# Block attention ahead of an MoE: scores taken per head on half of TensorE's rows, 128 queries of one head at a time, in a new order of units

## The chip, the core and the metric

The kernel runs on one core of a Trainium2 chip. The metric is device time in microseconds of one execution, from launch to end; before the change it was 1011.18 us, the median of three runs (1010.61 to 1013.1). TensorE (PE) multiplies and transposes, VectorE (DVE) and ScalarE (ACT) read its results from PSUM, GpSimd (POOL) works in SBUF alone, and SyncE (SP) issues nearly all DMAs.

## The reference

Three layers follow each other: attention with a mask in blocks of 64, a mixture of 8 experts in which each expert takes 288 tokens, and a bilinear layer. The change touches the first.

```python
B, H, S, D = 4, 8, 576, 64
scores = q @ k.T / sqrt(D)                  # per batch and head, 576 x 576
mask = (pos_q // 64) >= (pos_k // 64)       # nine blocks of 64; a block sees itself and those before
attn = softmax(where(mask, scores, -1e9))
x = (attn @ v)                              # to [B*S, H*D] = [2304, 512]
# then: experts relu(x @ w1[e]) @ w2[e] for the 288 tokens that each expert takes,
# then: (x @ w_a) * (x @ w_b) @ w_out
```

Precision is kept by splitting: a product in fp32 is made of three in the faster type fp32r, high by high, high by low and low by high, so `kh`, `kl` are the two parts of the transposed keys and `qh`, `ql` those of the queries. Transposes and the product with v stay in fp32.

## The kernel before

The attention works on 16 pairs of heads, one pair (`n`) per step, with the two heads' 64 features side by side on the 128 partitions. A pair's work is cut into units: `k`, `q`, `t` transpose keys and queries on PE and copy them out on ACT (lines 83 to 107); `sk`, `sp` split them on POOL (lines 114 to 120); `S0` to `S8` take the scores of one block of 64 queries, `E0` to `E8` their exponentials; `A0` to `A6` transpose the 25 tiles of 128x128 (line 172) and copy them to SBUF (line 174); `P0` to `P4` multiply with v (line 190); `ev` copies the result to `xT` (lines 195 and 196). `S` is three matmuls (line 149) and a maximum on DVE (line 150). Its stationary tile `qh[:,i,:]` is block-diagonal: the 64 queries of head 0 stand over the first 64 rows and those of head 1 over the others, with zeros elsewhere, so one matmul over all 128 rows gives 64 queries of both heads, and half of the array multiplies zeros. Blocks 0 and 1 are done in fp32 (line 137).

The order in which the units are issued is the string `SEQ`, walked once per step. `S` and `E` are of pair n, `A`, `P`, `ev` of pair n-1 and the transposes and splits of pair n+1, so a step overlaps three pairs. Each engine executes what it gets in that order. `w` stands for one piece of side work (constants for the routing, then the conversion of three weight arrays on DVE, three passes for each of 36 tiles, lines 797 to 801, with DMAs in and out), and `x` for a piece of what follows a finished batch of four pairs (`rr`, `lgm`, `lgt`, `first`: reciprocal sums and routing logits). PSUM's eight banks hold three `tr` tiles, three `s` tiles and one `pv` tile of two banks, which also takes the scores of the ninth block. The string `ACT` says which groups of `A` are copied by ACT; the others go to DVE.

After the last pair the routing of the first expert runs alone, and then the experts and the bilinear layer follow.

Of the kernel before, what the change touches and what calls it, by code (L numbers as in the profile page):

```python
# [13 lines left out]
ACT='46531'  # L14
# [3 lines left out]
SEQ='k A0 S0 e8 A1 S1 q E1 A2 w A3 S2 P0 t E0 E2 w w x A4 S3 E3 A5 w S6 S4 E4 P1 w sk x A6 w P2 P3 P4 ev E6 S5 E5 S7 S8 w E7 x sp'  # L18
def attention(ctx, tc, q, k, v, w_gate, xT, r_all, logits, idf, side, first):
# [3 lines left out]
    nc=tc.nc  # L23
# [3 lines left out]
    NB=S//64  # L27
    NC=B*S//128
    cst=ctx.enter_context(tc.tile_pool(name="acst",bufs=1))
    raw=ctx.enter_context(tc.tile_pool(name="araw",bufs=2))  # L30
    wk=ctx.enter_context(tc.tile_pool(name="awk",bufs=2))
    ps=ctx.enter_context(tc.tile_pool(name="aps",bufs=2,space=PSUM))
    QH,QL,QF,AA,VV=[],[],[],[],[]
    NF=2
    for i in range(2):
        t=cst.tile([128,NF,128],F32,name=f"qf{i}")
        nc.gpsimd.memset(t,0.0)
        QF.append(t)
        for l,nm in ((QH,"qh"),(QL,"ql")):
            t=cst.tile([128,NB,128],F32R,name=f"{nm}{i}")  # L40
            nc.gpsimd.memset(t.bitcast(F32),0.0)
            l.append(t)
    for i in range(2):
        t=cst.tile([128,25,128],F32,name=f"A{i}")
        AA.append(t)
    nc.vector.memset(AA[0],0.0)
    for i in range(4):
        t=cst.tile([128,5,2,64],F32,name=f"v{i}")
        nc.vector.memset(t[64:128,4],0.0)
        VV.append(t)  # L50
    one=cst.tile([128,1],F32,name="one")
    nc.gpsimd.memset(one,1.0)
    nc.scalar.activation(cst.tile([128,1],F32,name="tab"),one,AF.Exp)
    wg=cst.tile([128,HP,32],F32,name="wg")
    nc.gpsimd.memset(wg,0.0)
    L=cst.tile([128,NC,128],F32,name="L")
    RT=cst.tile([128,B,HP,NB],F32,name="RT")
    st={}
    off=[0]
    for i in range(NB): off.append(off[-1]+i//2+1)  # L60
    order=[(i,j) for j in range(5) for i in range(2*j,NB)]
    joff=[order.index((2*j,j)) for j in range(5)]

    def load(n):
        b,hp=divmod(n,HP)
        def ld(t,src):
            for h in range(2):
                nc.sync.dma_start(t[:,0:4,h,:],src[b,2*hp+h,0:512,:].rearrange("(i p) d -> p i d",p=128))
            nc.sync.dma_start(t[0:64,4,:,:],src[b,2*hp:2*hp+2,512:576,:].rearrange("h p d -> p h d"))
        for nm,src in (("k",k),("q",q)):  # L70
            t=raw.tile([128,5,2,64],F32,name=nm+"r")
            ld(t,src)
            st[nm,n]=t
        ld(VV[n%4],v)

    def t_units(n):
        def mk():
            st['kh',n]=wk.tile([128,S],F32R,name="kh")
            st['kl',n]=wk.tile([128,S],F32R,name="kl")
            st['qT',n]=wk.tile([128,S],F32,name="qT")  # L80
            st['kT',n]=wk.tile([128,S],F32,name="kT",bufs=2)
        def evk(p,a,b):
            nc.scalar.copy(st['kT',n][:,a:b],p)
        def first():
            if ('kh',n) not in st: mk()
        def km():
            first()
            p=ps.tile([128,512],F32,name="tr",bufs=3)
            for i in range(4):
                nc.tensor.transpose(p[:,128*i:128*i+128],st['k',n][:,i].rearrange("p h d -> p (h d)"),idf)  # L90
            evk(p,0,512)
        def tl():
            first()
            p=ps.tile([128,512],F32,name="tr",bufs=3)
            nc.tensor.transpose(p[:,0:64],st['k',n][0:64,4].rearrange("p h d -> p (h d)"),idf[0:64,0:64])
            nc.tensor.transpose(p[:,64:128],st['q',n][0:64,4].rearrange("p h d -> p (h d)"),idf[0:64,0:64])
            evk(p[:,0:64],512,576)
            nc.scalar.mul(st['qT',n][:,512:576],p[:,64:128],0.125)
        def qm():
            first()  # L100
            p=ps.tile([128,512],F32,name="tr",bufs=3)
            for i in range(4):
                nc.tensor.transpose(p[:,128*i:128*i+128],st['q',n][:,i].rearrange("p h d -> p (h d)"),idf)
            nc.scalar.mul(st['qT',n][:,0:512],p,0.125)
            for h in range(2):
                s=slice(64*h,64*h+64)
                nc.scalar.mul(QF[n%2][s,:,s],p[s,0:64*NF].rearrange("p (i d) -> p i d",d=64),0.125)
        def sp():
            qT=st.pop(('qT',n)); qh,ql=QH[n%2],QL[n%2]
            for h in range(2):  # L110
                s=slice(64*h,64*h+64)
                src=qT[s].rearrange("p (i d) -> p i d",d=64)
                eng=nc.vector if n==0 and h==0 else nc.gpsimd
                eng.tensor_tensor(qh[s,:,s],src,one[s,:,None].to_broadcast([64,NB,64]),op=ALU.mult)
                eng.tensor_tensor(ql[s,:,s],src,qh[s,:,s].bitcast(F32),op=ALU.subtract)
        def sk():
            kT=st['kT',n]; kh,kl=st['kh',n],st['kl',n]
            eng=nc.gpsimd if n else nc.vector
            eng.tensor_tensor(kh,kT,one.to_broadcast([128,S]),op=ALU.mult)
            eng.tensor_tensor(kl,kT,kh.bitcast(F32),op=ALU.subtract)  # L120
        return dict(q=qm,t=tl,sp=sp,k=km,sk=sk)

    def s_units(n):
        b,hp=divmod(n,HP)
        def grp(i):
            W=64*(i+1)
            def f():
                if i==0:
                    st['sm',n]=wk.tile([128,NB],F32,name="sm")
                    st['mx',n]=wk.tile([128,NB],F32,name="mx")  # L130
                mx=st['mx',n]
                kh,kl=st['kh',n],st['kl',n]
                qh,ql,qf,kT=QH[n%2],QL[n%2],QF[n%2],st['kT',n]
                if i<NF:
                    p=ps.tile([128,512],F32,name="s",bufs=3)
                    view=p[:,:W]
                    nc.tensor.matmul(p[:,:128],qf[:,i,:],kT[:,:128],start=True,stop=True)
                    parts=[]
                elif W<=512:
                    p=ps.tile([128,512],F32,name="s",bufs=3)  # L140
                    parts=[(p[:,:max(W,256)],0,max(W,256))]
                    view=p[:,:W]
                else:
                    p=ps.tile([128,2,512],F32,name="pv",bufs=1)
                    parts=[(p[:,c,:W//2],c*W//2,W//2) for c in range(2)]
                    view=p[:,:,:W//2]
# [3 lines left out]
                nc.vector.tensor_reduce(mx[:,i:i+1],view,axis=AX.X if W<=512 else AX.XY,op=ALU.max,negate=True)  # L150
                st['view',n,i]=view
            def g():
                A=AA[n%2]; sm=st['sm',n]; mx=st['mx',n]
                view=st.pop(('view',n,i))
                o=A[:,off[i]:off[i+1],:].rearrange("p a b -> p (a b)")[:,:W]
                if W>512: o=o.rearrange("p (a b) -> p a b",a=2)
                nc.scalar.activation(o,view,AF.Exp,bias=mx[:,i:i+1],accum_out=sm[:,i:i+1])  # L157
                if i==NB-1:
                    nc.vector.tensor_scalar(sm,sm,1e-9,None,op0=ALU.add)
                    nc.vector.reciprocal(RT[:,b,hp,:],sm)  # L160
            return f,g
        return [grp(i) for i in range(NB)]

    def at_units(n):
        def grp(g):
            def f():
                if g==0: st['AT',n]=wk.tile([128,2,25*64],F32,name="AT")
                A,AT=AA[n%2],st['AT',n]
                blk=order[4*g:4*g+4]; nb=len(blk)
                p=ps.tile([128,512],F32,name="tr",bufs=3)  # L170
                for m,(i,j) in enumerate(blk):
                    nc.tensor.transpose(p[:,128*m:128*m+128],A[:,off[i]+j,:],idf)  # L172
                o=AT[:,:,256*g:256*g+64*nb].rearrange("p h (i d) -> p h i d",d=64)
                (nc.scalar.copy if str(g) in ACT else nc.vector.tensor_copy)(o,p[:,:128*nb].rearrange("p (i h d) -> p h i d",h=2,d=64))
            return f
        return [grp(g) for g in range(7)]

    def pv_units(n):
        b,hp=divmod(n,HP)
        cut=[0,320,576]  # L180
        def main(j):
            def f():
                if j==0: st['pv',n]=ps.tile([128,2,512],F32,name="pv",bufs=1)
                p,AT,vv=st['pv',n],st['AT',n],VV[n%4]
                for c in range(2):
                    a,e=max(128*j,cut[c]),cut[c+1]
                    if a>=e: continue
                    for h in range(2):
                        o=64*joff[j]+a-128*j
# [51 lines left out]
    for u in ('k','q','t','sk','sp'): T[u]()  # L241
# [3 lines left out]
    for n in range(N+1):  # L245
        if n+2<N: load(n+2)
# [20 lines left out]
    for f in pend+batch_units(B-1): f()  # L267
# [590 lines left out]
```

## Time and profile before

| of the profiled execution | value |
|---|---|
| its own time | 1013.26 us |
| span from first to last instruction | 1011.5 us |
| mean granted clock of TensorE | 0.976 of 2.4 GHz |
| PE busy | 954.3 us, 94% |
| DVE busy | 711.2 us, 70% |
| ACT busy | 439.9 us, 43% |
| POOL busy | 206.4 us, 20% |

The profiled execution took 2.1 us more than the median of the runs. Its span is 1.8 us shorter than its time. The attention fills the first 231 us, the routing of the first expert lies at 231 to 285 us, and what remains is the experts and the bilinear layer, in which PE is the busy engine. A row's duration is the latency of one instruction; instructions of an engine overlap, so the cost of one in a stream is read from the distance between the starts of neighbours.

### The profile page before, as it was taken

The numbers are of one execution on the slowest core, as the hardware profiler recorded it, in microseconds if no ns is written. First come the engines' busy times: TensorE is split into PE (matmuls) and PEld (weight loads), VectorE is DVE, ScalarE is ACT, GpSimd is POOL, SyncE is SP. The second block draws the span as 40 slices with busy tenths as digits, with TensorE's granted clock in tenths as the row PEclk, the third lists the DMA queues.
The fourth block names the chain that finished last, engine by engine and source line by source line (L and its number), as shares of the span: only waits on it lengthen the run. The fifth ranks groups of instructions, "written<-read, shape, count | busy, mean of one in ns | idle before, by whom it ended". The sixth has DMA issues, their size and how long they took to land.

```text
span 1011.5 us, 20472 instructions
## 1 busy us (share of the span) xinstructions
PE 954.3 (94%) x7741; PEld 893.9 (88%) x7741; DVE 711.2 (70%) x1627; ACT 439.9 (43%) x1108; POOL 206.4 (20%) x215
## 2 busy tenths in 40 slices
PE   6998999988499999999999999999999999999996
PEld 5776877766398999999999999999999999999996
DVE  6889899896687876776767767766767776535421
ACT  5775777753363344225323522442253235325321
POOL 8766566622100020011001100200110011101001
PEclk9999899997599999999999999999999999999999
DMA  6687787633784245025304611440352046215300
GB/s 141 177 238 201 195 228 205 186 103 137 223 260 133 59 125 160 21 75 162 94 12 118 180 44 43 147 130 23 97 160 73 12 119 190 67 52 160 84 12 24
DMA packets 134563, 123.14 MB, mean 122 GB/s; under 512 B 64320, under 2 KB 97088, under 8 KB 134464
## 3 DMA queue, kind: packets, MB, share of 16 engines
q1 hardware_dynamic: 131392, 112.32, 38.8%
q0 software_dynamic: 3072, 9.51, 3.0%
q8 instruction: 61, 1.00, 0.4%
q14 instruction: 38, 0.31, 0.1%
HBM read 102.85 MB, written 18.95 MB: 120 GB/s over the span
## 4 chain that ended last, share of the span: by engine, by line
PE 80%; DVE 10%; DMA 5%; ACT 2%; issue 2%; POOL 1%; SPq 0%; POOLq 0%; DVEq 0%; ACTq 0%
PE h L637 13%; PE h L638 12%; PE h L639 12%; PE acc L638 8%; PE acc L637 8%; PE acc L639 8%; PE tr L172 4%; PE s L149 3%; PE pv L190 3%; DMA xo<-xs,idx 3%; PE m L438 2%; DVE mx L150 1%; PE pv L149 1%; PE h L746 1%; DVE cf L801 1%
## 5 line engine op out<-in xcount | busy, mean ns | idle before, releaser
L637 PE MATMUL acc<-th,spl 128*128 128x288 f32 x640 | 191.8, 300 | 0.4 <-ACT th L688 0.3
L638 PE MATMUL acc<-tl,spl 128*128 128x288 f32 x640 | 189.2, 296 | 0.5
L639 PE MATMUL acc<-th,spl 128*128 128x288 f32 x640 | 189.5, 296 | 0.0
L624 DVE TENSOR_TENSOR spl<-raw,spl 128x512 fp32r<-128x512 f32 x224 | 153.0, 689 | 29.3 <-ACT spl L623 23.3
L623 ACT CAST spl<-raw 128x512 fp32r<-128x512 f32 x224 | 137.4, 620 | 35.6 <-PE acc L639 28.8
L525 POOL DMA_INDIRECT xo<-xs,idx x24 | 25.6, 1067 | 492.2 <-DVE cg L534 448.1
L638 PEld LDWEIGHTS acc<-tl,spl 128*128 128x128 f32 x640 | 120.9, 189 | 1.7 <-DVE tl L689 1.5
L637 PEld LDWEIGHTS acc<-th,spl 128*128 128x128 f32 x640 | 120.6, 188 | 0.9 <-ACT th L688 0.9
L639 PEld LDWEIGHTS acc<-th,spl 128*128 128x128 f32 x640 | 120.5, 188 | 0.0
L688 ACT CAST th<-h 128x288 fp32r<-128x288 f32 x96 | 38.3, 399 | 182.3 <-DVE h L686 181.0
L637 PE MATMUL h<-y,wah 128*128 128x288 f32 x384 | 116.1, 302 | 0.0
L637 PE MATMUL h<-y,wbh 128*128 128x288 f32 x384 | 115.1, 300 | 0.0
L638 PE MATMUL h<-y,wbh 128*128 128x288 f32 x384 | 113.4, 295 | 0.0
L639 PE MATMUL h<-y,wal 128*128 128x288 f32 x384 | 113.4, 295 | 0.0
L638 PE MATMUL h<-y,wah 128*128 128x288 f32 x384 | 113.1, 295 | 0.0
L639 PE MATMUL h<-y,wbl 128*128 128x288 f32 x384 | 113.0, 294 | 0.0
L681 ACT COPY ta<-h 128x288 f32<-128x288 f32 x96 | 38.3, 399 | 158.8 <-PE h L639 158.8
L686 DVE TENSOR_TENSOR h<-h,ta 128x288 f32<-128x288 f32 x96 | 44.4, 463 | 87.9 <-PE h L639 85.9
L637 PE MATMUL h<-xh,spl 128*128 128x288 f32 x256 | 79.7, 311 | 3.4 <-ACT xh L570 3.4
L157 ACT ACTIVATE A<-s,mx 128x128 f32<-128x128 f32 (+7 forms) x128 | 64.0, 504 | 38.3 <-DVE mx L150 37.3
L638 PE MATMUL h<-xl,spl 128*128 128x288 f32 x256 | 76.8, 300 | 1.1 <-DVE xl L571 1.1
L639 PE MATMUL h<-xh,spl 128*128 128x288 f32 x256 | 76.8, 300 | 0.0
(213 smaller groups left out, 2186.5 us busy)
## 6 DMA issues: line engine op xcount, KB each, us to landing
raw<-in_moe_w_dram SPq DMA_DIRECT2D x128, 256.0 KB, 3.4
raw<-wo SPq DMA_DIRECT2D x96, 256.0 KB, 2.8
cw<-in_moe_w_a_dram SPq DMA_DIRECT2D x12, 512.0 KB, 4.9
cw<-in_moe_w_b_dram SPq DMA_DIRECT2D x12, 512.0 KB, 4.5
cw<-in_moe_w_out_dram SPq DMA_DIRECT2D x12, 512.0 KB, 4.3
xs<-spl SPq DMA_DIRECT2D x18, 260.0 KB, 2.3
kr<-in_k_dram SPq DMA_DIRECT2D x32, 128.0 KB, 4.3
qr<-in_q_dram SPq DMA_DIRECT2D x32, 128.0 KB, 3.7
```

Source lines behind the costliest of these rows:

```text
L149: nc.tensor.matmul(o,ww[:,i,:],kk[:,c:c+w],start=s0,stop=s1)
L157: nc.scalar.activation(o,view,AF.Exp,bias=mx[:,i:i+1],accum_out=sm[:,i:i+1])
L172: nc.tensor.transpose(p[:,128*m:128*m+128],A[:,off[i]+j,:],idf)
L190: nc.tensor.matmul(p[64*h:64*h+64,c,a-cut[c]:e-cut[c]],vv[:,j,h,:],AT[:,h,o:o+e-a],start=(j==0), stop=(j==(2 if c==0 else 4)),skip_group_c ...
L623: nc.scalar.copy(t[:,0,:],src)
L624: V.tensor_tensor(t[:,1,:],src,t[:,0,:].bitcast(F32),op=ALU.subtract)
L637: nc.tensor.matmul(p,wh,xh,start=s0,stop=False)
L638: nc.tensor.matmul(p,wh,xl,start=False,stop=False)
L639: nc.tensor.matmul(p,wl,xh,start=False,stop=s1)
L681: nc.scalar.copy(t,pa[:,:CAP])
L686: V.tensor_tensor(g,g,t,op=ALU.mult)
L688: later(1,lambda: nc.scalar.copy(gh,g))
```

## The change

The units are cut anew. A tile of scores is now 128 queries of one head (`t` = 0 to 3) against the keys up to its end. The two heads are two matmuls, each over 64 of the 128 rows of the array (`qq[s,...]`, `kk[s,...]` with `s` the partitions of head `h`), each into its own PSUM bank of one `s` tile; the first two tiles, 256 columns each, share the banks of one `s` tile. In the upper 64 queries the last block of keys is masked by one more matmul per head, in bf16, that adds -1e30. The last 64 queries of both heads stay together in a block-diagonal tile (`t` = 4, `Q8`, line 136 of the changed kernel), and POOL only copies these 64 columns. The keys and queries are transposed as five tiles of 128x128, the last half empty, into the `pv` tile; ACT writes the high part from PSUM and DVE subtracts it to give the low part. The sums are collected in `SM` and inverted once per batch. Six of seven groups of `A` are copied by ACT and `xT` by ACT alone. In the order string each unit now carries a lag: `S0.1` is the first score tile of the pair of the step before, `P0.3` is for the pair three steps back, so there are 19 steps for 16 pairs. PSUM holds two `s` tiles of two banks, two `tr` tiles and the `pv` tile. Loads run one step ahead, not two, and five pieces of side work come before the first step.

On PE, in a step in the middle of the attention, two score units and the transposes between them were, before (`qh`, `ql` are the block-diagonal queries, `kh`, `kl` the keys, `A` the exponentials):

```order
L149 MATMUL s<-kh,qh_116 128x256
L149 MATMUL s<-kl,qh_116 128x256
L149 MATMUL s<-kh,ql_118 128x256
L172 MATMUL tr<-idf,A_127 128x128 x4
L149 MATMUL s<-kh,qh_116 128x448
L149 MATMUL s<-kl,qh_116 128x448
L149 MATMUL s<-kh,ql_118 128x448
L149 MATMUL s<-kh,qh_116 128x320
```

In the changed kernel the units that follow the product with v are, on PE (`k_135` are keys as loaded, `mw`, `mv` the operands of the mask, `q8h` the block-diagonal rest):

```order
L193 MATMUL pv<-AT,v_146 64x64 x10
L164 MATMUL tr<-idf,A_133 128x128 x8
L86 MATMUL pv<-idf,k_136 128x128 x5
L114 MATMUL s<-kh,qh 128x384 x2
L114 MATMUL s<-kl,qh 128x384 x2
L118 LDWEIGHTS mw
L118 MATMUL s<-mv,mw 128x64
L114 MATMUL s<-kh,ql 128x384 x2
L164 MATMUL tr<-idf,A_133 128x128 x4
L136 MATMUL s<-kh,q8h_123 128x288 x2
```

Each matmul of a score is now a pair (x2), one per head, and the transposed keys go to the `pv` tile between the product with v and the next scores.

On ACT, around the copy of a pair's result to `xT`, the order was before:

```order
L174 COPY AT<-tr 128x2x64
L195 COPY xT<-pv 128x320
L157 ACTIVATE A_127,sm<-s,mx 128x448
L157 ACTIVATE A_127,sm<-s,mx 128x384
L157 ACTIVATE A_127,sm<-s,mx 128x512
L83 COPY kT<-tr 128x512
L157 ACTIVATE A_127,sm<-pv,mx 128x576
L174 COPY AT<-tr 128x2x256
L104 ACTIVATE qT<-tr 128x512
```

and it is now, for one whole step:

```order
L197 COPY xT<-pv 128x576
L175 COPY AT<-tr 128x2x2x128 x2
L91 CAST kh<-pv 128x576
L175 COPY AT<-tr 128x2x2x128
L148 ACTIVATE A_131,SM<-s,mx 128x384 x2
L96 ACTIVATE qh<-pv 128x576
L150 ACTIVATE A_131,SM<-s,mx 128x576
L175 COPY AT<-tr 128x2x256
L148 ACTIVATE A_131,SM<-s,mx 128x512 x2
L175 COPY AT<-tr 128x512
L148 ACTIVATE A_133,SM<-s,mx 128x128 x2
L148 ACTIVATE A_133,SM<-s,mx 128x256 x2
```

The splits (`kh`, `qh`) and the whole of `xT` stand in ACT's queue now, between copies that PE waits for and exponentials that free PE's score tiles.

The core of the diff:

```diff
-SEQ='k A0 S0 e8 A1 S1 q E1 A2 w A3 S2 P0 t E0 E2 w w x A4 S3 E3 A5 w S6 S4 E4 P1 w sk x A6 w P2 P3 P4 ev E6 S5 E5 S7 S8 w E7 x sp'
+SEQ=('S0.1 A5.3 w E0.1 A6.2 P0.3 w w w x E1.1 P1.3 w P2.3 w P3.3 P4.3 ev.3 A0.2 A2.2 k.0 S2.1 ks.0 A3.2 x E2.1 S4.1 '
+     'q.0 qs.0 E4.1 A4.2 A1.2 S3.1 E3.1 w')
-ACT='46531'
+ACT='012345'
...
-            eng.tensor_tensor(kh,kT,one.to_broadcast([128,S]),op=ALU.mult)
-            eng.tensor_tensor(kl,kT,kh.bitcast(F32),op=ALU.subtract)
+            nc.scalar.copy(kh,p)
+            nc.vector.tensor_tensor(kl,p,kh.bitcast(F32),op=ALU.subtract)
...
-                for ww,kk,s0,s1 in ((qh,kh,True,False),(qh,kl,False,False),(ql,kh,False,True)):
-                    for o,c,w in parts:
-                        nc.tensor.matmul(o,ww[:,i,:],kk[:,c:c+w],start=s0,stop=s1)
+            W=128*(t+1); w=max(W,256)
+            for i,(qq,kk) in enumerate(((qh,kh),(qh,kl),(ql,kh))):
+                for h in range(2):
+                    s=slice(64*h,64*h+64)
+                    nc.tensor.matmul(p[:,h,:w],qq[s,128*t:128*t+128],kk[s,0:w],start=i==0,stop=i==2)
+                if i==1:
+                    for h in range(2):
+                        s=slice(64*h,64*h+64)
+                        nc.tensor.matmul(p[:,h,W-64:W],mw[s],mv[s],start=False,stop=False)
...
-            nc.scalar.copy(xT[:,hp,b*S:b*S+320],p[:,0,:320])
-            nc.vector.tensor_copy(xT[:,hp,b*S+320:b*S+576],p[:,1,:256])
+            nc.scalar.copy(xT[:,hp,b*S:b*S+S],p[:,0:S])
```

## Rows read from the trace of the kernel before

**Rows 1.** Busy time by stretch: us, busy (instructions) per engine, clock, DMA.

```profile
core 0: us, PE busy (x) PEld busy (x) DVE busy (x) ACT busy (x) POOL busy (x), PEclk, DMA share, GB/s
32.00:231.00 199.00, 187.16 (x1497) 147.67 (x1500) 177.83 (x347) 138.72 (x438) 115.35 (x80) 0.98 0.67 187
100.00:110.00 10.00, 8.95 (x52) 8.10 (x53) 7.40 (x17) 5.75 (x18) 0.17 (x2) 0.68 0.38 96
285.00:1011.00 726.00, 709.46 (x5832) 697.70 (x5831) 473.19 (x1125) 262.64 (x578) 54.15 (x69) 1.00 0.33 96
```

**Rows 2.** Line 195, the copy to xT: ns min/median/max, first and last start in us.

```profile
L195 ACT COPY xT<-pv x16: 425/426/428, 32.8 to 230.2; 128x320 f32<-128x320 f32 x16
```

**Rows 3.** First fp32r score in the timeline: start us, us, engine, line.

```profile
12.75 0.55 PE L149 MATMUL s<-kh,qh 128*128 128x256 f32 x1
```

**Rows 4.** Timeline of PE, one step in the middle of the attention.

```profile
159.82 0.36 PE L149 MATMUL s<-kh,qh 128*128 128x256 f32 x1
...
162.15 0.37 PE L149 MATMUL s<-kh,qh 128*128 128x256 f32 x1
...
162.47 0.28 PE L149 MATMUL s<-kh,ql 128*128 128x256 f32 x1
162.59 0.60 PE L172 MATMUL tr<-idf,A 128*128 128x128 f32 x4
162.94 0.45 PE L149 MATMUL s<-kh,qh 128*128 128x448 f32 x1
...
164.17 0.98 PE L190 MATMUL pv<-AT,v 128*64 128x192 f32 x8
...
166.47 0.44 PE L149 MATMUL s<-kh,qh 128*128 128x384 f32 x1
...
167.80 0.42 PE L149 MATMUL pv<-kh,qh 128*128 128x288 f32 x2
...
168.59 0.60 PE L90 MATMUL tr<-idf,kr 128*128 128x128 f32 x4
169.02 0.60 PE L172 MATMUL tr<-idf,A 128*128 128x128 f32 x4
169.46 0.39 PE L137 MATMUL s<-kT,qf 128*128 128x128 f32 x2
169.68 0.60 PE L172 MATMUL tr<-idf,A 128*128 128x128 f32 x4
...
171.65 0.37 PE L149 MATMUL s<-kh,qh 128*128 128x256 f32 x1
```

**Rows 5.** Timeline of PE's weight loads, two loads for 448-column scores.

```profile
162.91 0.19 PEld L149 LDWEIGHTS s<-kh,qh 128*128 128x128 f32 x1
163.03 0.19 PEld L149 LDWEIGHTS s<-kl,qh 128*128 128x128 f32 x1
```

**Rows 6.** Timeline of ACT in the same step.

```profile
168.72 0.69 ACT L157 ACTIVATE A<-s,mx 128x512 f32<-128x512 f32 x1
...
169.40 0.58 ACT L83 COPY kT<-tr 128x512 f32<-128x512 f32 x1
169.87 0.76 ACT L157 ACTIVATE A<-pv,mx 128x576 f32<-128x576 f32 x1
...
170.60 0.59 ACT L174 COPY AT<-tr 128x512 f32<-128x512 f32 x1
```

**Rows 7.** Line 801, third pass of the conversion: ns min/median/max.

```profile
L801 DVE SCALAR_TENSOR_TENSOR cf<-cw,cf x36: 677/691/1923, 38.3 to 227.7; 128x512 int32<-128x512 int32 x36
```

**Rows 8.** Groups of DVE's instructions, 0 to 232 us: busy us, mean ns.

```profile
L801 DVE SCALAR_TENSOR_TENSOR cf<-cw,cf 128x512 int32<-128x512 int32 x36 | 33.6, 934 | 0.3
...
L174 DVE COPY AT<-tr 128x512 f32<-128x512 f32 x32 | 21.9, 686 | 3.1 <-PE tr L172 2.8
...
L150 DVE TENSOR_REDUCE mx<-pv 128x1 f32<-128x576 f32 x16 | 12.1, 757 | 2.2 <-PE pv L149 0.8
```

**Rows 9.** Timeline of PE, ninth block's scores after a wait; idle time in brackets.

```profile
101.05 0.85 PE L149 MATMUL pv<-kh,qh 128*128 128x288 f32 x2 [2.72 <-DVE xT L196]
```

More of the change, by code (lines that the diff above doesn't have):

```diff
@@ L56, in attention @@
     L=cst.tile([128,NC,128],F32,name="L")
-    RT=cst.tile([128,B,HP,NB],F32,name="RT")
+    SM=cst.tile([128,B,HP,9],F32,name="SM")
     st={}
[L59 to L62, printed above, removed]
+    J=(0,4,7,9)
+    aof=lambda t,h: t*(t+1)+h*(t+1) if t<NT else 20
     def load(n):
@@ L82, in evk @@
[L82 to L115, printed above, removed]
@@ new lines, in X @@
+        def X(t):
+            def g():
+                A=AA[n%2].rearrange("p a b -> p (a b)"); mx=st['mx',n]
+                p=views.pop(t)
+                if t<NT:
+                    W=128*(t+1)
+                    for h in range(2):
+                        o=128*aof(t,h)
+                        nc.scalar.activation(A[:,o:o+W],p[:,h],AF.Exp,bias=mx[:,2*t+h:2*t+h+1],accum_out=SM[:,b,hp,2*t+h:2*t+h+1])
+                else:
+                    nc.scalar.activation(A[:,2560:3136].rearrange("p (c a) -> p c a",c=2),p,AF.Exp,bias=mx[:,8:9],accum_out=SM[:,b,hp,8:9])
+            return g
@@ L164, in at_units @@
+        return [S(t) for t in (0,2,3,4)],[X(t) for t in range(NT+1)]
     def at_units(n):
@@ L233, in lgt @@
             return f
-        c0,c1=b*S//128,(b+1)*S//128
+        c1=(b+1)*S//128
         return [rr,lgm(0),lgm(1)]+[lgt(c,min(4,c1-c)) for c in range(c0,c1,4)]+[lambda: first(logits,c0,c1)]
-    load(0); load(1)
+    load(0)
+    for _ in range(5): next(side)
     for h in range(2):
         nc.sync.dma_start(wg[64*h:64*h+64,:,8*h:8*h+8],w_gate.rearrange("(c h p) e -> h p c e",p=64,h=2)[h])
-    T=t_units(0)
-    for u in ('k','q','t','sk','sp'): T[u]()
-    nc.gpsimd.memset(AA[1],0.0)
-    pend=[]
@@ L267, in attention @@
-    for f in pend+batch_units(B-1): f()
+    pend=[]; units={}
+    for step in range(N+LAG):
+        if step+1<N: load(step+1)
+        if step==0: next(side)
+        for u,_,l in seq:
+            if u=='w':
+                if step: next(side,None)
+            elif u=='x':
+                if pend: pend.pop(0)()
+            else:
+                n=step-int(l)
+                if not 0<=n<N: continue
+                if n not in units:
+                    d=t_units(n)
+                    s_,e_=s_units(n)
+                    for t,f in zip((0,2,3,4),s_): d[f'S{t}']=f
+                    for t,f in enumerate(e_): d[f'E{t}']=f
+                    for t,f in enumerate(at_units(n)): d[f'A{t}']=f
+                    *p,e=pv_units(n)
+                    for j,f in enumerate(p): d[f'P{j}']=f
+                    d['ev']=e
+                    units[n]=d
+                units[n].pop(u)()
+                if u=='ev' and n%HP==HP-1: pend+=batch_units(n//HP)
@@ L268, in attention @@
+    assert not any(units.values())
+    for f in pend: f()
     for _ in side: pass
```

232 lines of the change are left out of this document (114 added, 118 removed).

## The prediction, made before the changed kernel ran

> **What bounds the kernel now.** I read the busy time by stretch first. In the last 726 us PE is busy for 709 and runs at full clock; nothing of that code is touched, so the change can only pay or cost in the attention [rows 1]. The attention is a pipeline of 16 pairs of heads. The copy of a pair's result to `xT` starts at 32.8 us for the first pair and at 230.2 us for the last, so a pair takes (230.2-32.8)/15 = 13.16 us [rows 2]. Then the timeline of PE. From the first score of one step at 159.82 to the same score of the next at 171.65 PE runs nearly without a gap: 11.83 us [rows 4]. That is PE's own work per pair. The other 1.33 us per pair are the pieces of finished batches, of which I take 0.5 us on PE, and waits. In the stretch of 32 to 231 us PE is busy for 187 of 199 us, DVE for 178, ACT for 139 and POOL for 115 [rows 1]. So PE bounds it, with DVE right behind; PE's longest waits are for DVE, as the one of 2.72 us before the ninth block's scores [rows 9].
>
> DVE's load is partly not its own. The third pass of the conversion has a median of 691 ns but a maximum of 1923 [rows 7], and its 36 instances sum to 33.6 us [rows 8], 8.8 more than 36 medians. The long ones lie beside POOL's splits in the timeline; I take it that the two engines hold each other up.
>
> **The change, part by part, per pair.** *Scores on PE.* Starts in the timeline give the old cost: a group of three matmuls of 256 columns 0.44 us (162.15 to 162.59), twice; 448 and 320 together 1.23 (162.94 to 164.17); 384 and 512 together 1.33 (166.47 to 167.80); the ninth block 0.79 (167.80 to 168.59); the two fp32 blocks 0.22 each (169.46 to 169.68) [rows 4]. The ninth block stays as it is. So 0.88+1.23+1.33+0.44 = 3.88 us go. The new scores are 24 matmuls in 12 pairs; each pair has the width 256, 256, 384 or 512, three times, 4224 columns in all. The ninth block's 1728 columns in 0.79 us give 0.457 ns a column. If the two halves of a pair run side by side, the pairs take 4224 x 0.457 = 1.93 us; if one after the other, 3.86. Between them lies a third price: two weight loads that nothing keeps apart start 0.12 us from each other [rows 5], and 24 loads in turn would be 2.88 us. No row of before shows two halves of the rows at work together. I take 1.93, since the nearest rows are the products with v, in which the two heads stand on halves of the columns: 192 and 256 columns of each head, two passes of fp32, issued at 164.17. To these are added 0.08 us on entering a score unit (0.44 less three times 0.12), three times, 0.24; and 8 matmuls of the mask, from 0.03 (64 columns) to 0.12 (a load) each, for which I take 0.4 together. Ten whole transposes in place of eight and two halves I cost at nothing. PE thus has 3.88 - (1.93+0.24+0.4) = 1.31 us less per pair side by side, 0.36 less if the loads set the pace, 0.62 more if the halves go one after the other. PE's work becomes 10.5, 11.5 or 12.45 us, and 0.5 for the batches.
>
> Here a rule speaks against the change. The Trainium skill, "TensorE: Matmul & The Clock Gate", section "LDWEIGHTS (loading the stationary operand)", says that a load's time goes by its columns and not by its rows, P/1.2 ns; an estimate from it is 107 ns for 128 columns, close to the 0.12 us above, and two half-height loads would then cost twice one whole load. The skill's "TensorEngine Tiling (Array Packing)", section "Key Properties", says the opposite of what follows from that: tiles load and multiply in parallel. By the first the sum would be that of the rival on loads below, by the second my own.
>
> *DVE.* Two copies of `AT` of 686 ns [rows 8], the copy of half of `xT`, and the work on the sums in every pair go; two splits of 576 columns come, which I price at 757 ns each, as the maximum over 576 columns of PSUM [rows 8]. That is near nothing, on balance below zero. What counts is POOL: its splits vanish but for four small copies, and with them, as I take it, DVE's long passes, 8.8/16 = 0.55 us per pair in the third pass alone. DVE's 178 us in 199 are 11.8 per 13.16; it ends between 10 and 11 us and leaves the second place. Were the passes as long as before, DVE would need 11.5 us, still under the step that I come to.
>
> *ACT.* It gets two more copies of `AT` and all of `xT`, and the splits' high parts in place of its copies of keys and queries. From its starts: an exponential of 512 columns takes 0.68 us, of 576 0.73, a copy of 512 columns 0.47 [rows 6], so 0.78 ns a column. The new exponentials are two each of 128, 256, 384, 512 columns (0.38, 0.48, 0.58, 0.68) and one of 576: 4.97 us; six copies 2.82; three operations of 576 columns at 0.52, 1.56. Sum 9.35 us per pair.
>
> *The order.* No engine is full now, so the chain through them sets the step. I walked one step by hand from these durations, with 0.1 to 0.2 us from one engine's result to the next engine's start. From the copy to `xT` on, ACT copies two groups, then the keys' high part; it waits 0.75 us for `A3`, because PE takes the scores of `S2` first; 0.3 us for `q`, because PE waits with `q.0` until DVE has read the keys out of the `pv` tile, behind the maximum of `S2`; 0.65 us for the maximum of `S3`, 1024 columns. ACT's queue then runs on through `A5`, `E0`, `E1` to the next copy to `xT`: 9.35 + 1.7 = 11.1 us. PE waits in it about half a microsecond. With the batches' 0.5 us and 0.4 us for waits that the walk doesn't see I take 12.0 us.
>
> *Beginning and end.* The first fp32r score of before starts at 12.75 us [rows 3]. After, DVE does the constants and one conversion pass, which waits for a 512 KB load, ahead of the first keys' split, so I leave it at 12.5. The first step has only scores (8.5 us, set by DVE and ACT), the second lacks the products with v (10.5), 13 are full (156.0), then three run out: 9.5, 5.5 and 4. The last copy to `xT` ends at 206.5 us, 24 us before that of 230.2. The three lags thus cost the ramp, and the gain is mostly in the 13 full steps, 15 us, and in the first pair, whose step of blocks and splits before was slow.
>
> **Sum.** The profiled execution took 1013.26 us, 1011.5 of them its span; less 24 that is 989. The median of the runs is 2.1 us lower, so I predict 987.
>
> **Rivals.** *Loads set the pace.* PE's work is 11.5 + 0.5, and a step 12.6: 13 x 0.6 = 8 us more, 995. For it speaks that one engine loads all weights; against it that transposes with a load each keep 0.11 us (four in 0.44, 169.02 to 169.46 [rows 4]) while a pair of 256 columns leaves the same time to two loads on different rows.
>
> *The halves run one after the other.* The change then doesn't do what it says: PE has 12.45 + 0.5 and with waits a step of 13.45, 13 x 1.45 = 19 us over my sum and 2 in the ramp: 1008, no change.
>
> *The chain has no slack to lose.* If batches and the rest hide in the walk's gaps, a step is 11.1: 12 us less, 975.
>
> *Slower: PE waits for ACT at the one `pv` tile.* The product with v, the keys' and the queries' transposes now take turns in it, and between them stands ACT's copy to `xT`, in a queue that has got the splits and six groups of copies. If ACT comes late there by the 2.72 us that PE waited for the same tile once before [rows 9], each of 13 steps pays it: 35 us, 1022. After that wait the pair of 288 columns took 0.85 us, twice the 0.42 of an undisturbed one [rows 4, 9], and the granted clock was 0.68 in that stretch of 10 us [rows 1], between the levels of 2.4 and 1.2 GHz, so it would hardly be cheaper. It decides from 24/13 = 1.85 us per step on. Against it: the walk puts two groups of transposes between, and finds ACT 0.9 us late at most.
>
> **How the numbers follow.** My forecast has 0.48, for itself 978 to 997; the loads 0.18, the halves in turn 0.10, the shorter step 0.12, the late ACT 0.12. The range reaches down past the shorter step and up to the halves in turn: 972 to 1007. A measurement of this kernel tells 0.3%, 3 us, from no change. Faster are the forecast, the shorter step, the loads and a quarter of the halves in turn: 0.81. Within 3 us lie most of the halves in turn: 0.08. Slower is the late ACT, less a little: 0.11.
>
> **What would show it.** Starts of a pair of 512 columns less than 0.05 us apart, and pairs 0.12 to 0.25 us from each other, show the halves side by side; 0.24 us for pairs of any width, the loads; twice the width, the halves in turn. The conversion passes should lie at their medians, with POOL nearly idle. The copies to `xT` should follow each other every 12 us, the last near 206, and ACT should be the engine that PE waits for. A distance over 13 us, or a granted clock below 0.9 in the middle of the attention, makes the prediction wrong; so does any change of more than 3 us after the attention.

## The result and the profile after

The changed kernel took 1026.56 us (median of 4 runs, 1024.32 to 1026.82), the kernel before on the same chip 1011.11 us (4 runs). The ratio is 1.0139, with a 95% interval of 1.0121 to 1.0156: slower by 15 us, where 987 us and a range up to 1007 were predicted.

The profiled execution took 1026.82 us, 1025.0 of them its span, 13.5 more than the span before. First the busy time by stretch (us, busy time and instructions of each engine, granted clock as a share of 2.4 GHz, DMA share, GB/s); these answer to [rows 1]:

```profile
core 0: us, PE busy (x) PEld busy (x) DVE busy (x) ACT busy (x) POOL busy (x), PEclk, DMA share, GB/s
32.00:231.00 199.00, 173.75 (x1632) 127.74 (x1633) 139.67 (x246) 141.96 (x391) 13.01 (x56) 0.95 0.65 181
60.00:70.00 10.00, 5.96 (x45) 4.64 (x44) 4.66 (x7) 3.85 (x11) 0.93 (x4) 0.83 0.89 236
298.00:1024.00 726.00, 710.27 (x5840) 698.70 (x5839) 474.84 (x1127) 263.93 (x580) 54.22 (x69) 1.00 0.33 97
```

The last 726 us are as before, PE busy for 710. All of the loss lies in the attention. The stretch of 32 to 231 us holds less of it than before, since its last copy now comes 14.5 us later. Taken whole, from 0 to 232 us before and from 0 to 246 us after, the attention keeps PE busy for 203 us instead of 210, DVE for 160 instead of 201, ACT for 161 instead of 155 and POOL for 21 instead of 143. In the stretch shown PE is idle for 25 us of 199. So the work became smaller, as planned, and waiting took its place. The copy to `xT` of the 16 pairs, against [rows 2]:

```profile
L197 ACT COPY xT<-pv x16: 638/649/676, 44.4 to 244.7; 128x576 f32<-128x576 f32 x16
```

The first is 11.6 us later than before, the last 14.5. Between the copies lie, in us: 12.4, 16.6, 11.4, 14.6, 13.7, 11.5, 12.1, 20.5, 13.0, 11.5, 17.1, 16.3, 13.0, 9.6, 6.9. The best steps take 11.45, less than the 11.83 of [rows 4]; five take 14 to 21. (The 12.0 predicted is a mean that includes the batches; it is taken up below.) One of the bad places, in the order of time; SPq is SP issuing DMAs, and the bracket at a row's end is the engine's idle time before it and what ended it:

```profile
51.15 1.26 SPq L72 DMA_DIRECT2D k<-in_k_dram  x2
...
55.76 0.68 DVE L805 SCALAR_TENSOR_TENSOR cf<-cw,cf 128x512 int32<-128x512 int32 x1
...
58.18 0.69 DVE L805 SCALAR_TENSOR_TENSOR cf<-cw,cf 128x512 int32<-128x512 int32 x1
...
59.39 0.61 SPq L73 DMA_DIRECT2D v<-in_v_dram  x1
...
60.10 0.54 SPq L806 DMA_DIRECT2D wa<-cf  x1
...
62.41 0.43 DVE L801 TENSOR_SCALAR cf<-cw 128x512 int32<-128x512 int32 x1 [3.54 <-DMA wa<-cf]
62.75 0.95 DVE L121 TENSOR_REDUCE mx<-s 128x2 f32<-128x768 f32 x1
63.62 0.75 DVE L92 TENSOR_TENSOR kl<-pv,kh 128x576 fp32r<-128x576 f32 x1
63.73 0.58 ACT L148 ACTIVATE A<-s,mx 128x384 f32<-128x384 f32 x1 [3.47 <-DVE mx L121]
...
64.47 0.87 PE L86 MATMUL pv<-idf,q 128*128 128x128 f32 x5 [4.04 <-issue]
```

Read it from the end. PE waits 4 us before it transposes the queries, because DVE has not read the keys out of the same `pv` tile; that reading (L92) ends at 64.37, although the page can only say "issue". ACT waits 3.5 us for a maximum. Both stand on DVE behind the conversion pass at 62.41, and this waits for the buffer `cf`, of which there are two. The tile that last held it was finished at 56.44, but its store was issued only at 60.10, 3.7 us later: SP first issued the nine loads of the next pair, from 51.15 to 60.00. From the issue to the waiting pass another 2.3 us went by. Afterwards the five transposes take 0.87 us where a quiet step has 0.74. The granted clock of the 10 us is 0.83, between the two levels of 2.4 and 1.2 GHz; from 64.9 to 68.3 it is 0.50, the lower level. The trace has four such stretches in the attention, 20.5 us together; the trace of the kernel before has one, of 6.8 us. The same chain stands at 142.25, where the wait is 3.98 us and the store came 3.3 us after the pass that it waited for.

The three conversion passes before the attention's end, busy us and mean ns, then the idle time before them; they answer to [rows 7, 8]:

```profile
L805 DVE SCALAR_TENSOR_TENSOR cf<-cw,cf 128x512 int32<-128x512 int32 x36 | 24.8, 688 | 0.7
L803 DVE SCALAR_TENSOR_TENSOR cf<-cw,cf 128x512 int32<-128x512 int32 x36 | 24.7, 687 | 0.7
L801 DVE TENSOR_SCALAR cf<-cw 128x512 int32<-128x512 int32 x36 | 15.2, 424 | 28.5 <-DMA wa<-cf 11.7 <-DMA wb<-cf 8.7 <-DMA cw<-in_moe_w_a_dram 4.7
```

The passes run at their undisturbed time, 688 ns against 934 in [rows 8]. But DVE sat idle for 28.5 us before the first of them: 23.8 us for stores (`wa`, `wb` and 3.4 for `wo`) and 4.7 once for the load of a weight tile.

### The profile page after: what moved, and what is told of

Its sections match the earlier page's. It is cut to its first block, busy times and chain, and to the rows that moved or that the text cites. A ratio compares the mean times of both kernels' runs of the same rounds, so it can differ in the third digit from the quotient of the medians.

```text
span 1025.0 us, 20740 instructions
## 1 busy us (share of the span) xinstructions
PE 947.1 (92%) x7965; PEld 875.9 (85%) x7965; DVE 669.8 (65%) x1535; ACT 446.8 (44%) x1060; POOL 82.5 (8%) x192
## 4 chain that ended last, share of the span: by engine, by line
PE 81%; DVE 6%; DMA 4%; issue 3%; ACT 3%; SPq 1%; POOL 1%; ACTq 0%; POOLq 0%; DVEq 0%
PE h L641 13%; PE h L642 12%; PE h L643 12%; PE acc L642 8%; PE acc L641 8%; PE acc L643 8%; PE s L114 4%; PE tr L164 3%; PE pv L188 3%; DMA xo<-xs,idx 2%; PE pv L86 2%; PE m L442 2%; PE s L136 1%; DVE mx L121 1%; ACT A L148 1%
## 5 line engine op out<-in xcount | busy, mean ns | idle before, releaser
L148 ACT ACTIVATE A<-s,mx 128x128 f32<-128x128 f32 (+3 forms) x128 | 66.4, 533 | 44.3 <-DVE mx L121 44.2
L641 PEld LDWEIGHTS h<-y,wah 128*128 128x128 f32 x384 | 72.4, 189 | 2.8 <-issue 2.7
```

The source lines that it names most:

```text
L148: nc.scalar.activation(A[:,o:o+W],p[:,h],AF.Exp,bias=mx[:,2*t+h:2*t+h+1],accum_out=SM[:,b,hp,2*t+h:2*t+h+1])
L641: nc.tensor.matmul(p,wh,xh,start=s0,stop=False)
```

## The experiments

Theory A: the loss is DVE standing before a conversion pass whose buffer is not back, with maxima and splits queued behind it. Rivals: the start, the pieces of a finished batch, and PE's own work.

**Four buffers.**

```diff
-        f=pool.tile([128,512],I32,name="cf",bufs=2)
+        f=pool.tile([128,512],I32,name="cf",bufs=4)
```

> Edit: the changed kernel with four buffers for a converted tile (cf) instead of two; nothing else. Theory A (SyncE's queue is in order; about 6 us of issuing the next pair's nine loads stands between a converted tile's store and the conversion pass that needs the buffer back, so VectorE stands still and the maxima behind it, too): VectorE's waits for the stores of cf, about 24 us in all, go, with the clock that falls after them; the longest distance between two copies to xT falls from 20.5 us to under 14, and the time from 1026.6 to 995-1005 us. Theory B (the order of the units itself stalls: ScalarE late at the one pv tile, and TensorE's transposes of the reciprocal sums behind VectorE): waits move to other releasers and the time stays within 5 us of 1026.

1005.06 us, ratio to the kernel before 0.9926 (0.9896 to 0.9955). The same rows in this run, first the copies to `xT`:

```profile
L197 ACT COPY xT<-pv x16: 639/659/676, 39.1 to 218.9; 128x576 f32<-128x576 f32 x16
```

and the first pass with the idle time before it:

```profile
L801 DVE TENSOR_SCALAR cf<-cw 128x512 int32<-128x512 int32 x36 | 15.2, 421 | 6.9 <-DMA cw<-in_moe_w_a_dram 6.6 <-DMA cw<-in_moe_w_b_dram 0.3
```

All waits for stores are gone, and 21.5 us come back for one number. The execution shown took 1001.32 us, the fastest of six (up to 1008.60), and in it the granted clock is 1.00 through the attention. Theory A is shown. The distances are now regular: 11.45 to 11.5, but 14.6 and 13.0 in two steps behind each batch, so the longest is 14.7, where under 14 was expected.

**The same four buffers in the kernel before** (the same line there).

> Edit: the kernel before with four buffers for cf instead of two. Theory A: the kernel before pays for the same queue, but less, since its side work is spread over the step: 1003-1009 us against 1011. Theory B: no change, within 2 us of 1011.

1012.98 us, 0.9999 (0.9976 to 1.0021): nothing, and the expected gain missed. The 2.4 us of store waits that went were not on its path. The buffer count is thus no gain in itself; it matters where the new order brings the passes together.

**Loads later**: SP gets the next pair's loads ahead of `P3`, when six of the step's seven `w` are through, instead of at the step's start.

```diff
-        if step+1<N: load(step+1)
         if step==0: next(side)
         for u,_,l in seq:
+            if u=='P3' and step+1<N: load(step+1)
```

> Edit: the changed kernel with the nine loads of the next pair issued at P3, behind six of the step's seven pieces of side work, instead of at the step's start; still two buffers for cf. Theory A: the stores of cf no longer stand behind the loads, so the waits go as with four buffers: 995-1008 us. A rival within A (two buffers are too few for the side work in a bunch, wherever the loads stand): 1015-1026 us. Theory B: within 5 us of 1026.

1008.97 us, 0.9958 (0.9937 to 0.9979), just above the range expected. DVE's waits for stores fall from 23.8 to 9.0 us, with two buffers. So most of them came from the place of the stores behind the loads.

**Side work spread over the step**: the loads at the step's start and two buffers, as in the change; only the seven `w` stand farther apart.

```diff
-SEQ=('S0.1 A5.3 w E0.1 A6.2 P0.3 w w w x E1.1 P1.3 w P2.3 w P3.3 P4.3 ev.3 A0.2 A2.2 k.0 S2.1 ks.0 A3.2 x E2.1 S4.1 '
-     'q.0 qs.0 E4.1 A4.2 A1.2 S3.1 E3.1 w')
+SEQ=('S0.1 A5.3 w E0.1 A6.2 P0.3 w x E1.1 P1.3 P2.3 w P3.3 P4.3 ev.3 A0.2 A2.2 w k.0 S2.1 ks.0 A3.2 w x E2.1 S4.1 '
+     'q.0 qs.0 w E4.1 A4.2 A1.2 S3.1 E3.1 w')
```

> Edit: the changed kernel, two cf buffers and the loads at the step's start as they were, but the seven pieces of side work spread over the step (behind A5, P0, P2, A2, A3, qs and E3) instead of six of them between A5 and P2. Theory: a converted tile's buffer is then asked back about 10 us later, after the 6 us of loads and the 2.4 us of the store are over, so most of VectorE's 24 us of waits for stores go: 1003-1010 us. If two buffers are too few whatever the spacing, 1018-1026 us.

1014.12 us, 1.002 (1.0 to 1.004). The waits for stores are 6.0 us, yet only 12 of the 21.5 us come back: less than expected, as three of the steps behind batches still take 15.4, 16.9 and 18.4 us; in the two longer ones the granted clock is 0.50 for 3.4 and 6.8 us. With the loads later more came back, 17.6 us, though 9.0 us of store waits were left, so the sum of these waits does not by itself give the time. Bunching is a condition of the loss, as the loads are.

**Stores issued by POOL** (two buffers).

```diff
-        nc.sync.dma_start(dst,f.bitcast(F32))
+        nc.gpsimd.dma_start(dst,f.bitcast(F32))
```

> The changed kernel with its two buffers kept; only the stores of converted tiles are issued by POOL, which is nearly idle, and no longer by SP behind the nine loads. Theory A (what costs is the place of the store in SP's queue, and the number of buffers only hides it): DVE's waits for stores, 24 us in the changed kernel, fall under 6; the copies to xT are 11.5 to 12 us apart outside a batch's two steps; 1003 to 1011 us. Theory B (the store itself is slow, 2.0 us at least from issue to landing, so that with two buffers a bunch of passes waits wherever it is issued): the waits stay above 12 us, and the time above 1016. Unknown: what POOL needs to issue a store, and whether that holds DVE up; by the row of POOL's activity beside the passes (691 to 1923 ns) it could take back a few us.

1047.75 us, 1.0337 (1.0296 to 1.0378): worse than the change itself. The first pass and its idle time:

```profile
L801 DVE TENSOR_SCALAR cf<-cw 128x512 int32<-128x512 int32 x36 | 15.3, 424 | 46.8 <-DMA wa<-cf 16.7 <-DMA wb<-cf 14.1 <-DMA wo<-cf 11.1
```

The stores no longer stand behind loads, but from issue to landing they now take a median of 4.7 us, where SP's took 2.9. In a bunch DVE comes back to a buffer about 2.4 us after it has finished with it (from 56.44 to 58.87 in the place above). A store that lands in 2 to 3 us fits or nearly does, one that first waits 3.7 us in SP's queue does not, and one that takes 4.7 does not either. The place in the queue is therefore not the whole cause, as Theory A said it here: it is the buffer's whole way back, of which the queue was the larger part in the change. The Trainium skill, "Perfetto Trace Analysis", section "DMA Optimizations", says that it may make sense to give loads to one engine and stores to another; here, with POOL as the second, the ratio went from 1.0139 to 1.0337, so this case went the other way. No run tried another engine.

**No conversion pass ahead of the first step.**

```diff
     for step in range(N+LAG):
         if step+1<N: load(step+1)
-        if step==0: next(side)
```

> Edit: the changed kernel without the piece of side work in step 0, so that VectorE splits the first keys without waiting for a 512 KB load of weights. If the start is a loss of its own, the first score's second matmul comes 3 to 5 us earlier and the time is 1021-1024 us; if the start only shifts what waits later, it stays at 1026 within 2 us.

1021.87 us, 1.0096 (1.0065 to 1.0128). The rows of the beginning of the changed kernel show what was aimed at, to be held against [rows 3]:

```profile
8.03 0.58 PE L114 MATMUL s<-kh,qh 64*128 64x256 f32 x2 [0.74 <-ACT qh L96]
...
10.24 0.43 DVE L801 TENSOR_SCALAR cf<-cw 128x512 int32<-128x512 int32 x1 [4.74 <-DMA cw<-in_moe_w_a_dram]
10.59 0.75 DVE L92 TENSOR_TENSOR kl<-pv,kh 128x576 fp32r<-128x576 f32 x1
...
11.39 0.29 PEld L114 LDWEIGHTS s<-kl,qh 64*128 64x128 f32 x2 [3.08 <-DVE kl L92]
```

The first product could start at 8.03, 4.7 us earlier than in [rows 3], but the next waits until 11.39 for the keys' low part, which DVE holds behind a pass that waits for its load. With this pass taken away alone the second product started at 8.39, 3.0 us earlier, but the first copy to `xT` at 45.6 us instead of 44.4: later store waits took the time. That the time fell by 4.7 us is therefore not shown to come from the start.

**Queue and start together**: four buffers, loads at `P3`, and no side work in the first two steps.

```diff
-                if step: next(side,None)
+                if step>1: next(side,None)
```

> Edit: the changed kernel with four cf buffers, the next pair's loads at P3, no side work in step 0 and none in step 1. With four buffers alone the copies to xT started at 39.1 us and then went every 11.45 us except around a batch. If the late start there comes from VectorE standing before weight loads that have not landed, the first copy to xT comes 3 to 6 us earlier and the time is 999-1003 us against 1005; if it comes from the lag of three steps alone, the first copy stays at 38-39 us and the time at 1005. The loads at P3 should change nothing more once there are four buffers.

1001.01 us, 0.9883 (0.9866 to 0.99); the first copy to `xT` starts at 35.1 us, 4 us earlier than with four buffers alone, and the time is 4 us lower. The second product now starts at 8.62, not at 11.39:

```profile
8.62 0.42 PE L114 MATMUL s<-kl,qh 64*128 64x256 f32 x2
```

In the two profiled executions the last copy to `xT` comes only 0.5 us earlier, at 218.4 instead of 218.9. They differ in the clock too: with four buffers alone it stayed at 1.00 through the attention, and here it fell in two of the three batches, as the next experiment shows.

**The batch's pieces moved.** To the last edit is added: the `x` go behind `ev` and behind `S4`, and the reciprocal of the sums becomes a piece of its own, ahead of their transposes.

```diff
-        def rr():
-            R=wk.tile([128,HP,9],F32,name="R")
+        def ra():
+            R=st['R']=wk.tile([128,HP,9],F32,name="R")
             nc.vector.tensor_scalar(R,SM[:,b],1e-9,None,op0=ALU.add)
             nc.vector.reciprocal(R,R)
+        def rr():
+            R=st['R']
```

> Edit: as queue_and_start, and the pieces of a finished batch stand behind ev and behind S4 instead of behind P0 and A3, with VectorE's part of the reciprocal sums as a piece of its own ahead of TensorE's. With four buffers a batch lengthened two steps from 11.45 to 14.6 and 13.0 us, 4.7 us for each of three batches. If that is TensorE waiting for a tr tile that ScalarE still has to copy, and for VectorE's reciprocals, those two steps come to under 13 and 12.5 us and the time is 5 to 9 us below queue_and_start; if it is the pieces' own work on a step without slack, it stays within 2 us of it.

991.25 us, 0.9791 (0.9774 to 0.9808), and the clock in the attention is 1.00. What it removes is seen in the run with four buffers, in a step of 14.6 us:

```profile
76.74 0.75 DVE L92 TENSOR_TENSOR kl<-pv,kh 128x576 fp32r<-128x576 f32 x1
...
77.61 0.38 DVE L207 RECIPROCAL R<-R 128x36 f32<-128x36 f32 x1
...
78.14 0.31 PE L212 MATMUL tr<-R,idf 128*64 128x32 f32 x4 [1.73 <-DVE R L207]
...
79.45 0.71 PE L86 MATMUL pv<-idf,q 128*128 128x128 f32 x5
...
80.25 0.65 ACT L96 ACTIVATE qh<-pv 128x576 fp32r<-128x576 f32 x1 [2.08 <-PE pv L86]
```

PE waits 1.7 us for the reciprocal, which stands on DVE behind the keys' split, and with it wait the ninth block's scores and the queries, so ACT idles for 2.1. In the run with queue and start together the two steps take 16.2 and 13.0 us in two of the three batches, and 14.6 and 13.0 in the third. In the longer step the wait for the reciprocal is again 1.73 us, but behind it the granted clock is 0.50 from 75.5 to 78.9 us, and the five transposes above take 1.24 us instead of 0.71:

```profile
75.50 1.24 PE L86 MATMUL pv<-idf,q 128*128 128x128 f32 x5
```

The same wait was thus followed by the upper level in one execution and by the lower in another. With the pieces moved, the three steps that a batch touches take 11.7, 12.4 and 12.7 us.

**The same, and the side work spread.**

> Edit: as batch_pieces_moved, and the side work spread: five pieces before P4, one behind A2, one behind qs and the last behind E3 (eight in a step instead of seven). With four buffers the spacing should no longer matter for stores; VectorE's queue ahead of the maxima of the first score tiles is shorter: 986-992 us against 991. More than 994 us would show that pieces between A2 and E4 delay the splits that TensorE waits for.

989.29 us, 0.9774 (0.9741 to 0.9808): not to be told from the run before it. With four buffers the bunching costs no more. (The string has four `w` ahead of `P4` and three behind it; the expectation counts otherwise.)

**All rows in each score matmul** (four buffers). Each matmul takes all 128 rows and so adds up the scores of both heads; the count of matmuls stays.

```diff
-                    nc.tensor.matmul(p[:,h,:w],qq[s,128*t:128*t+128],kk[s,0:w],start=i==0,stop=i==2)
+                    nc.tensor.matmul(p[:,h,:w],qq[:,128*t:128*t+128],kk[:,0:w],start=i==0,stop=i==2)
...
-                        nc.tensor.matmul(p[:,h,W-64:W],mw[s],mv[s],start=False,stop=False)
+                        nc.tensor.matmul(p[:,h,W-64:W],mw,mv,start=False,stop=False)
```

> Edit: the changed kernel with four cf buffers, and each score matmul of the four tiles of 128 queries takes all 128 rows instead of one head's 64. It computes the sum of both heads' scores in place of each head's own, with the same number of matmuls, columns and operands. The matmuls of a pair can no longer run side by side: TensorE's scores take 1.9 us more per step. In heads_one_after_other the start times showed the halves overlapping although they were issued one after the other, so that run did not remove the overlap; this one does. If TensorE has no slack for it, a step grows from 11.45 to about 13 us and the time to 1020-1035 us; if the chain through VectorE and ScalarE hides it, 1005-1010 us.

1022.76 us, 1.0083 (1.0051 to 1.0115), 17.7 more than with four buffers. One pair of heads takes 12.86 us in place of 11.45. The timeline of PE, scores of a 512-column tile, first in the changed kernel (the columns are start, us, then line, operation and shape; x2 are the two heads):

```profile
120.62 0.36 PE L114 MATMUL s<-kh,ql 64*128 64x256 f32 x2
120.92 0.77 PE L171 MATMUL tr<-idf,A 128*128 128x128 f32 x5
...
130.29 0.50 PE L114 MATMUL s<-kh,qh 64*128 64x512 f32 x2
130.63 0.40 PE L114 MATMUL s<-kl,qh 64*128 64x512 f32 x2
130.87 0.20 PE L118 MATMUL s<-mv,mw 64*128 64x64 bf16 x2
...
131.23 0.28 PE L114 MATMUL s<-kh,qh 64*128 64x256 f32 x2
131.34 0.28 PE L114 MATMUL s<-kl,qh 64*128 64x256 f32 x2
...
131.50 0.37 PE L114 MATMUL s<-kh,ql 64*128 64x256 f32 x2
131.70 0.28 PE L114 MATMUL s<-kh,qh 64*128 64x256 f32 x2
```

and with all rows:

```profile
129.70 0.72 PE L114 MATMUL s<-kh,qh 128*128 128x512 f32 x2
130.26 0.62 PE L114 MATMUL s<-kl,qh 128*128 128x512 f32 x2
130.72 0.23 PE L118 MATMUL s<-mv,mw 128*128 128x64 bf16 x2
...
131.33 0.40 PE L114 MATMUL s<-kh,qh 128*128 128x256 f32 x2
```

The tile takes 0.94 us on halves and 1.63 on all rows, and the second product is followed after 0.24 us against 0.46. The halves do run side by side, and this is worth 1.4 us a pair of heads, 12.86 less 11.45. The loads don't set the pace either: two matmuls of 256 columns are followed by the next two after 0.11 us (131.23 to 131.34), where two loads in turn had been priced at 0.24.

**Heads one after the other** (four buffers): the program issues all matmuls of one head's tile before those of the other.

```diff
-            for i,(qq,kk) in enumerate(((qh,kh),(qh,kl),(ql,kh))):
-                for h in range(2):
-                    s=slice(64*h,64*h+64)
+            for h in range(2):
+                s=slice(64*h,64*h+64)
+                for i,(qq,kk) in enumerate(((qh,kh),(qh,kl),(ql,kh))):
```

> Edit: the changed kernel with four cf buffers, and in each score tile all three products of head 0 ahead of those of head 1, so that neighbours use the same half of the array's rows; the same matmuls otherwise. If neighbours on different halves run side by side, a tile of 512 columns now takes twice as long, TensorE's work per step rises by about 1.9 us, and the time by 20 to 30 us over the 1005 of four buffers; if the halves never overlapped, or TensorE has that much slack, it stays within 3 us.

1007.17 us, 0.9947 (0.993 to 0.9963), about the time of four buffers alone. The edit was to take the overlap away, and it did not:

```profile
121.05 0.51 PE L114 MATMUL s<-kh,qh 64*128 64x512 f32 x2
121.39 0.40 PE L114 MATMUL s<-kl,qh 64*128 64x512 f32 x2
...
121.97 0.39 PE L114 MATMUL s<-kh,qh 64*128 64x256 f32 x2
```

The second head's first product starts with that of the first head, 13 ns behind it in the records, although three matmuls of the first head stand between them in the program, and the tile takes 0.92 us (121.05 to 121.97). The run says nothing on what the overlap is worth.

**POOL kept busy** (four buffers): four products of 128x576 in SBUF per pair, whose result nobody reads.

```diff
+            for _ in range(4): nc.gpsimd.tensor_tensor(pz[1],pz[0],one.to_broadcast([128,S]),op=ALU.mult)
```

> Edit: the changed kernel with four cf buffers, and four more elementwise operations of 128x576 per pair on GpSimd, on a scratch tile that nothing reads, about 5 us per step. If GpSimd and VectorE hold each other up, the conversion's passes, which lie at 0.69 us with GpSimd idle, reach maxima near 1.9 us as in the kernel before, VectorE's busy time in the attention grows by 8 to 20 us, and the time by 3 to 15 us; if not, the passes stay below 0.75 us and the time within 2 us of 1005.

1022.23 us, 1.009 (1.0073 to 1.0108), 17 more than without. The passes and their mean ns (the third pass, L808, has the same 939):

```profile
L806 DVE SCALAR_TENSOR_TENSOR cf<-cw,cf 128x512 int32<-128x512 int32 x36 | 33.8, 939 | 0.6
L804 DVE TENSOR_SCALAR cf<-cw 128x512 int32<-128x512 int32 x36 | 23.9, 664 | 4.8 <-DMA cw<-in_moe_w_a_dram 4.7
```

With four buffers alone the same three passes take 688, 688 and 421 ns; the 939 stands beside the 934 of [rows 8]. That POOL's splits stretched DVE's passes in the kernel before was taken on trust in the prediction; here it is shown for products of 128x576 on POOL, and the 17 us are more than the 3 to 15 expected.

## Why the prediction was wrong

**The step that failed** is the order, and in it the words that DVE gets "near nothing, on balance below zero". The walk went through PE, ACT and DVE; it took the conversion passes as time on DVE, of which there was enough, and not as instructions with a wait. It never went past SP's queue, which the change rearranged: loads one step ahead, nine issues of about 6 to 9 us in all, and six of seven `w` between `A5` and `P3`, right behind them. The prediction's only allowance for it was the 0.4 us per step for waits that the walk doesn't see, 5 us in 13 steps. The wait that this makes is 23.8 us on DVE, the sum of what follows from it 21.5 us (four buffers).

**The slower rival** had the right shape and the wrong place. It let PE wait at the `pv` tile for ACT; there PE waited for ACT twice, 1.3 us in all. Where it waited long at that tile, as the 4.0 us at 64.47, it was for DVE's read of the keys. The half clock behind a long wait, taken from [rows 1, 9], came as it said.

**The second term mis-sized** is the batches' 0.5 us per pair. They took (14.6 + 13.0 - 2 x 11.45) = 4.7 us per batch, 1.2 per pair, and 6.3 per batch where the clock fell, because the reciprocal of the sums stood on the path of three engines. Moving them gave back 9.8 us.

**The beginning** came as it was described: the first product could start at 8.03, but the second waited until 11.39 for the pass that waits for its load, and the prediction had put the first score at 12.5 for that reason. It took this pass as part of the start and not as a thing to move. The pass and what follows it cost 4 us: the first copy to `xT` starts at 39.1 us with four buffers and at 35.1 without side work in the first two steps.

**What held.** The halves run side by side. A quiet tile of 512 columns and the two of 256 and the one of 384 behind it take 0.94, 0.47, 0.57 and 0.85 us, 2.8 in all, against 2.57 worked out. A quiet step is 11.45 us. It answers to the walk's 11.1, as the 12.0 also holds 0.5 for the batches and 0.4 for waits that the walk doesn't see. The walk's three waits of ACT, and PE's wait before the queries, are there in a quiet step with four buffers:

```profile
115.59 0.59 ACT L175 COPY AT<-tr 128x512 f32<-128x512 f32 x1 [0.75 <-PE tr L164]
...
115.89 0.75 DVE L92 TENSOR_TENSOR kl<-pv,kh 128x576 fp32r<-128x576 f32 x1
...
116.74 0.74 PE L86 MATMUL pv<-idf,q 128*128 128x128 f32 x5 [0.39 <-PE s L136]
...
117.57 0.65 ACT L96 ACTIVATE qh<-pv 128x576 fp32r<-128x576 f32 x1 [0.25 <-PE pv L86]
...
120.68 0.69 ACT L148 ACTIVATE A<-s,mx 128x512 f32<-128x512 f32 x1 [0.77 <-DVE mx L121]
```

ACT waits 0.75, 0.25 and 0.77 us, against 0.75, 0.3 and 0.65 walked. PE's 0.39 us end when DVE has read the keys, at 116.64, as in the walk, though the page names PE itself. From 113.0 to 124.5 us ACT is busy for 9.7 us and PE for 11.1; so PE's own work is 11.1 us, where 10.5 were worked out, and both engines' chains fill the step. That PE has no slack in it is what the run on all rows shows: the step grew by the 1.4 us that the scores grew. That ACT would be the engine that PE waits for did not hold: with four buffers its longest waits, 5.2 us in three, are for DVE's reciprocal. The passes lie at their medians, and nothing changed behind the attention. With the three terms taken out one after the other, 21.5, 4.0 and 9.8 us, the changed kernel comes to 991.25, inside the forecast's own 978 to 997, though the 4.0 had not been counted in its sum. In that run the first 13 distances between copies are 11.94 us on average, against 12.0, and the last copy starts at 207.7, against 206. In part this is luck: the walk was 0.35 us short, and the 0.4 set aside for waits unseen happened to cover it. The gain that was worked out can be had; the change as written spent it, and 15 us more, on waits.

What is left open: how the 23.8 us of waits divide between the loads in SP's queue, the bunching and the store's own way. Each of the first two, taken away alone, removes most of them, 14.8 and 17.8 us. Open, too, is how much of the loss is the lower clock that follows the waits, as no run holds the clock. An estimate: if 3.4 us at the lower level cost 1.6 us, as in a batch's step (16.2 less 14.6), the 20.5 us cost about 10, and the 6.8 before the change about 3.

## What to carry to other kernels

Whoever walks a schedule by hand walks the queues of the DMAs too: for each buffer that an engine writes again, note when its last reader is issued, what that reader's queue holds before it, and when it lands, beside when the engine wants it back. A piece of side work that waits is not hidden by idle time on its engine, because what the main path needs stands behind it in the same queue. Before blaming a large change, try a deeper buffer at the place of the longest wait: one number gave back 21.5 of the 39.6 us between prediction and result, and nothing in the kernel before, where these waits came to 2.4 us in all.

## What the runs showed of the hardware

Matmuls on the two halves of the rows start 13 ns apart also where the program has three others of the first half between them, so in the records TensorE does not keep the issued order across halves. The Trainium skill, "TensorE: Matmul & The Clock Gate", section "The mechanism", says that matmuls start and end in the program's order; the trace of that run shows otherwise for the starts.

A change from whole rows to halves and back costs time. From the five transposes of the keys to the first score product are 0.64 us when the product stands on halves (four buffers), and 0.46 when it takes all rows:

```profile
113.41 0.71 PE L86 MATMUL pv<-idf,k 128*128 128x128 f32 x5
114.05 0.45 PE L114 MATMUL s<-kh,qh 64*128 64x384 f32 x2
```

```profile
124.66 0.71 PE L86 MATMUL pv<-idf,k 128*128 128x128 f32 x5
125.12 0.59 PE L114 MATMUL s<-kh,qh 128*128 128x384 f32 x2
```

The way back is cheaper: from the last products on halves to the next transposes are 0.30 us (120.62 to 120.92), and to another pair on halves 0.20 (131.50 to 131.70). A step goes to the halves and back twice, so an estimate from these numbers is some 0.5 us of its 11.45. The prediction had 0.08 us for entering a score unit, from rows on which no such change happens.

A store of 256 KB that POOL issued landed after a median of 4.7 us, one that SP issued after 2.9 in the changed kernel and 3.6 with the side work spread. One of POOL's issues took 0.54 us, where the medians of SP's three groups of stores are 0.33 to 0.38.
